# The activation h - tanh(h) by its short form alone, with a range test by row sums and a general path behind it

## The chip, the cores and the metric

The kernel runs on one core of a Trainium2 chip. The metric is the time of one execution on the device in microseconds, as the median of several runs. A profile holds one execution; its span runs from the first instruction to the last. PE is TensorE (PEld its weight loads), ACT ScalarE, DVE VectorE, POOL GpSimd, SP the engine that issues the DMAs.

## The reference

Three stages follow each other on the same 4608 tokens (8 batches of 576). First an attention with 32 packed keys for each of 8 heads, then a layer with a cubic-like activation, then a layer in which each token goes to one of 8 experts:

```python
def sm_attn(qq, kk, vv):
    s = scale * np.matmul(qq, kk.transpose(0, 1, 3, 2))
    ...
p_packed = sm_attn(p, k, v)
x = sm_attn(q, p_packed, p_packed)      # as 4608 x 512
h = x @ w_in                            # 512 -> 2048
g = h - np.tanh(h)
x = g @ w_out                           # 2048 -> 512
logits = x @ w_gate + modality_bias[modality_id]
e_idx = np.argmax(logits, axis=1)
...
out[mask] = gate_w[mask, None] * (np.maximum(x[mask] @ w1[e], 0.0) @ w2[e])
```

The inputs are normal draws with a seed that defaults to 0. v has a spread of 0.1, and q, k and p have 0.8. w_in and w_out are float64 in memory.

## The kernel before

**Tiling.** The tokens are worked on in 16 half batches of 288 tokens (HW = 288), number hb. h is held transposed: 128 of the 2048 hidden columns on the partitions, 288 tokens along the row. A half batch has 16 such tiles f (NF = 16). One step of the first part is a *slot* n: one tile f of one half batch. There are 256 of them; the first 32 serve half batches 0 and 1 in alternating halves, while the weights are still being converted.

**A slot.** `gemm1` (L720) multiplies m, the product of the packed values and w_in, with a2, the second attention's weights, into a PSUM tile `h` (two buffers). From slot 32 on both operands are split into a high and a low part, and `mm3` (L96) makes three matmuls of each product. `chain` (L731) makes g out of h. `gsplit` (L754) splits g into gh and gl. `gemm2` (L765), three slots later (LAG = 3), multiplies them with w_out into four PSUM tiles `acc`. At the end of a half batch `evac` (L779) copies acc out, splits it and stores it to DRAM (x2_hi, x2_lo). `logits_pe`, `route_in` and `routing` compute the expert of each token.

**The chain.** For small u = h^2, h - tanh(h) is PA (exp(-PK u) + PB) u h, the short form. ACT computes u (L741), tanh(h) (L742), a mask that is nonzero where u > U_THR = 0.0775 (L743) and the exponential (L744). DVE computes h - tanh(h) (L745), the two steps of the short form (L747, L749), and selects the first where the mask is set (L751). u, qq, th and mk have one buffer each. The low part gl is computed on POOL in seven of sixteen slots and on DVE in the others (L761, L762).

**Beside the slots.** The loops of the main part give each slot a list of further work by number (`at_pe`, `at_pre`, `at_post`, `at_cv`): the attention of the next batch (`attention`, L247), the m tiles of the next batch (`m_pe`, L211, eight per batch, with loads of `ws` three slots ahead), and in the first slots the conversion of the float64 weights (`conv_a`, L159: two steps on DVE, three on ACT, one on POOL; `conv_b`, L187). Within these lists a planner orders each engine's instructions; TensorE's small products all go through one PSUM tile `at` (AT). Almost all DMAs are issued on SP's queue.

**The second layer.** From slot 256 on, `gemm1b`, `relu` and `gemm2b` compute the expert of token 0 for all tokens. `flags_a`, `flags_pe` and `flags_b` (L611 to L646) count, for each other expert and half batch, whether a token chose it. `other_experts` (L649) reads that total at the very end (n_any, L652) and branches (L653): if it is not zero, it goes through all experts, and for each with tokens through all half batches with tokens (`other_half`, L680), computes this expert in full precision and writes the rows that chose it.

## Time and profile before

| | us |
|---|---|
| median of 3 runs | 1284.95 |
| lowest, highest run | 1284.23, 1285.18 |
| the profiled execution | 1284.04 |
| its span | 1282.3 |

The granted TensorE clock is 0.983 of full speed over the span. The page gives each engine's busy time and its share of the span; a group row gives line, engine, operation, tile and shape, then busy time, mean ns of one, and the idle time just before with what ended it. Windows split the span in time.

### The profile page before, as it was taken

How to read it: one execution, taken by the hardware profiler on the slowest of the kernel's cores; microseconds unless marked ns; L12 is line 12 of the kernel's file. 1: busy time of each engine (PE TensorE's matmuls, PEld its weight loads, DVE VectorE, ACT ScalarE, POOL GpSimd, SP SyncE). 2: the span in 40 equal slices, each digit the busy share in tenths (PEclk: the TensorE clock that was granted, in tenths of full speed). 3: DMA queues.
4: the chain of work that ended last, by engine and by line, in shares of the span. 5: the costliest groups of instructions: out<-in, count | busy, mean ns of one | idle time of the engine just before them, and what ended most of it. 6: DMA issues, size and time to landing. Idle time of an engine off the chain costs nothing.

```text
span 1282.3 us, 25934 instructions
## 1 busy us (share of the span) xinstructions
PE 1210.1 (94%) x9762; PEld 1049.7 (82%) x9763; DVE 838.4 (65%) x1941; ACT 710.3 (55%) x1832; POOL 166.3 (13%) x174
## 2 busy tenths in 40 slices
PE   5688889999999999999999999999999999999996
PEld 2455668889889889979979978989899999999995
DVE  4987999898998898998898897884111111111111
ACT  3888867678678678678677777772111111111111
POOL 1322211121111111111111122240000000000000
PEclk7799899999999999999999999999999999999998
DMA  8766344454354344344345126212122222222201
GB/s 241 213 201 197 104 131 118 106 131 121 73 129 119 73 125 124 73 118 128 73 108 139 39 83 194 79 51 74 63 83 67 82 61 76 64 65 83 66 17 35
DMA packets 189843, 132.36 MB, mean 103 GB/s; under 512 B 122640, under 2 KB 167696, under 8 KB 189712
## 3 DMA queue, kind: packets, MB, share of 16 engines
q1 hardware_dynamic: 189712, 130.65, 36.6%
q8 instruction: 78, 1.28, 0.4%
q14 instruction: 53, 0.43, 0.1%
HBM read 98.10 MB, written 32.51 MB: 102 GB/s over the span
## 4 chain that ended last, share of the span: by engine, by line
PE 68%; DVE 16%; issue 7%; ACT 4%; DMA 3%; POOL 2%; SPq 0%; POOLq 0%; DVEq 0%; ACTq 0%
PE acc L98 12%; PE acc L100 12%; PE acc L99 11%; PE h L98 9%; PE h L99 8%; PE h L100 8%; PE at L202 2%; DVE gs L749 2%; DVE th L745 2%; DVE gs L751 2%; DVE gl L762 1%; PE at L340 1%; DVE qq L747 1%; DMA w1s<-in_moe_w_dram 1%; DVE s L466 1%
## 5 line engine op out<-in xcount | busy, mean ns | idle before, releaser
L98 PE MATMUL acc<-gh,wo_hi 128*128 128x288 f32 x960 | 293.9, 308 | 6.4 <-ACT gh L760 4.0
L100 PE MATMUL acc<-gl,wo_hi 128*128 128x288 f32 x960 | 277.0, 298 | 5.4 <-DVE gl L762 2.9
L99 PE MATMUL acc<-gh,wo_lo 128*128 128x288 f32 x960 | 281.9, 295 | 0.0
L98 PEld LDWEIGHTS acc<-gh,wo_hi 128*128 128x128 f32 x960 | 180.4, 188 | 42.2 <-ACT u L741 13.2
L100 PEld LDWEIGHTS acc<-gl,wo_hi 128*128 128x128 f32 x960 | 177.6, 188 | 13.5 <-DVE gl L762 6.2
L99 PEld LDWEIGHTS acc<-gh,wo_lo 128*128 128x128 f32 x960 | 180.6, 188 | 0.4 <-issue 0.2
L100 PE MATMUL h<-xbl,w1h 128*128 128x256 f32 x576 | 162.3, 282 | 0.0
L99 PE MATMUL h<-xbh,w1l 128*128 128x256 f32 x576 | 162.1, 281 | 0.0
L98 PE MATMUL h<-xbh,w1h 128*128 128x256 f32 x576 | 161.5, 280 | 0.0
L762 POOL TENSOR_TENSOR gl<-gs,gh 128x288 fp32r<-128x288 f32 x105 | 85.7, 817 | 569.4 <-ACT gh L760 398.4
L745 DVE TENSOR_TENSOR th<-h,th 128x288 f32<-128x288 f32 x256 | 114.8, 449 | 53.8 <-ACT mk L743 51.2
L751 DVE COPY_PREDICATED gs<-mk,th 128x288 f32<-128x288 int32 x256 | 140.1, 547 | 2.6
L98 PE MATMUL h<-ah,mh 128*128 128x288 f32 x448 | 135.2, 302 | 6.5 <-DVE gs L749 6.5
L741 ACT ACTIVATE u<-h 128x288 f32<-128x288 f32 x256 | 106.0, 414 | 63.3 <-PE h L100 40.8
L863 DVE SCALAR_TENSOR_TENSOR bl<-h,bh 128x256 fp32r<-128x256 f32 x72 | 30.6, 425 | 164.0 <-ACT bh L862 163.9
L99 PE MATMUL h<-ah,ml 128*128 128x288 f32 x448 | 132.2, 295 | 0.0
L100 PE MATMUL h<-al,mh 128*128 128x288 f32 x448 | 131.8, 294 | 0.0
L747 DVE SCALAR_TENSOR_TENSOR qq<-qq,u 128x288 f32<-128x288 f32 x256 | 122.7, 479 | 12.8 <-ACT qq L744 9.9
L744 ACT ACTIVATE qq<-u 128x288 f32<-128x288 f32 x256 | 114.6, 448 | 27.1 <-DVE gs L749 21.9
L760 ACT ACTIVATE gh<-gs 128x288 fp32r<-128x288 f32 x240 | 107.6, 449 | 35.3 <-PE acc L99 33.8
L742 ACT ACTIVATE th<-h 128x288 f32<-128x288 f32 x256 | 104.6, 409 | 34.9 <-DVE gs L751 32.2
L862 ACT ACTIVATE bh<-h 128x256 fp32r<-128x256 f32 x72 | 27.6, 384 | 171.3 <-PE h L100 169.8
(163 smaller groups left out, 2426.4 us busy)
## 6 DMA issues: line engine op xcount, KB each, us to landing
ws<-w_in_v SPq DMA_DIRECT2D x56, 512.0 KB
nat<-in_v_dram SPq DMA_DIRECT2D x16, 576.0 KB
x_hi<-x2h SPq DMA_DIRECT2D x16, 576.0 KB
x_lo<-x2l SPq DMA_DIRECT2D x16, 576.0 KB
xbh<-x_hi SPq DMA_DIRECT2D x18, 512.0 KB
xbl<-x_lo SPq DMA_DIRECT2D x18, 512.0 KB
raw<-in_moe_w_in_dram SPq DMA_DIRECT2D x32, 256.0 KB
raw<-in_moe_w_out_dram SPq DMA_DIRECT2D x16, 512.0 KB
```

Of the source, the lines that this page charges most:

```text
L98: nc.tensor.matmul(out=ps, lhsT=ah, rhs=bh, start=first, stop=False)
L99: nc.tensor.matmul(out=ps, lhsT=al, rhs=bh, start=False, stop=False)
L100: nc.tensor.matmul(out=ps, lhsT=ah, rhs=bl, start=False, stop=last)
L741: nc.scalar.activation(out=u, in_=ps, func=ACTF.Square)
L742: nc.scalar.activation(out=th, in_=ps, func=ACTF.Tanh)
L744: nc.scalar.activation(out=qq, in_=u, func=ACTF.Exp, scale=-PK)
L745: nc.vector.tensor_tensor(out=th, in0=ps, in1=th, op=ALU.subtract)
L747: nc.vector.scalar_tensor_tensor(out=qq, in0=qq, scalar=PB, in1=u, op0=ALU.add, op1=ALU.mult)
L751: nc.vector.copy_predicated(gs, mk, th)
L760: nc.scalar.activation(out=gh, in_=gs, func=ACTF.Copy)
L762: eng.tensor_tensor(out=gl, in0=gs, in1=f32(gh), op=ALU.subtract)
L863: nc.vector.scalar_tensor_tensor(out=gl, in0=ps, scalar=0.0, in1=f32(gh), op0=ALU.max, op1=ALU.subtract)
```

## The change

The chain loses tanh, mask, subtraction and selection. u and qq get two buffers each in the place of th and mk. The square's activation also sums its row into a column of a new tile usum (128 x 256), one column for each slot. The split's low part is always on DVE. After the last slot, `flags_a` takes the largest row sum of each partition and compares it with U_THR; `flags_pe` counts the partitions over it, and `flags_b` puts the count into the flags and adds it to the total that is branched on. For the general path, a2, ppT and, in the path itself, the logits are kept in DRAM (a2_all, pp_all, lg_all).

If the count is not zero, `redo` runs ahead of the experts' loop. It converts w_out again and loops over the batches. In each it loads ppT and w_in, computes m, and in `redo_half` computes both halves in full precision with tanh, mask and selection, writes x anew and keeps the logits. Then it routes anew and sets the flags with `every=True`, which counts all experts, the one of token 0 too; the loop behind it then computes all of them.

The diff, without the arguments of the buffers in `relu` and lines that only move:

```diff
@@ -60,6 +60,11 @@
...
+    a2_d = nc.dram_tensor("a2_all", [NHB, 128, 2 * HW], F32, kind="Internal").ap()
+    pp_d = nc.dram_tensor("pp_all", [B, 128, 128], F32, kind="Internal").ap()
+    lg_d = nc.dram_tensor("lg_all", [NHB, 32, 9 * NE], F32, kind="Internal").ap()
@@ -81,6 +86,8 @@
...
     flags = const.tile([1, NE + 1, NHB + 1], I32, name="flags")
+    ones_b = const.tile([128, 1], F32, name="ones_b")
+    usum = const.tile([128, NHB * NF], F32, name="usum")
@@ -106,6 +113,7 @@
...
         nc.vector.memset(ones, 1.0)
+        nc.vector.memset(ones_b, 1.0)
@@ -173,6 +181,8 @@
...
             v = early.tile([128, 512], F32, name="wv", tag="wv", bufs=6)
+        elif key[0] == 2:
+            v = wv[key]
         elif key[1] < NWH // 2:
@@ -425,7 +435,9 @@
...
             t = ppT[b] = ap.tile([128, 4, 32], F32, name="ppT", tag="ppT", bufs=2)
-            nc.scalar.activation(out=t.rearrange("p h j -> p (h j)"), in_=ps[:, 0, 128:256], func=ACTF.Copy)
+            t = t.rearrange("p h j -> p (h j)")
+            nc.scalar.activation(out=t, in_=ps[:, 0, 128:256], func=ACTF.Copy)
+            nc.sync.dma_start(out=pp_d[b], in_=t)
@@ -490,6 +502,7 @@
...
             r["a2", half] = t
+            nc.sync.dma_start(out=a2_d[2 * b + half], in_=t.rearrange("p g c -> p (g c)"))
@@ -620,37 +633,133 @@
...
+        t = evp.tile([128, 1], F32, name="big", tag="big")
+        nc.vector.tensor_reduce(out=t, in_=usum, axis=AX.X, op=ALU.max)
+        yield
+        nc.vector.tensor_scalar(out=t, in0=t, scalar1=U_THR, scalar2=None, op0=ALU.is_gt)
+        yield
+        fl["big"] = t
...
         fl["ps"] = AT[0:1, 0, 0:NE * NHB]
+        nc.tensor.matmul(out=AT[0:1, 1, 0:1], lhsT=ones_b, rhs=fl["big"], start=True, stop=True)
         nc.tensor.matmul(
...
-    def flags_b():
-        other = evp.tile([1, NE], F32, name="other", tag="rt_m")
-        nc.vector.tensor_tensor(
-            out=other, in0=em8[0:1, :], in1=idx_t[0:1, 0:1].to_broadcast([1, NE]), op=ALU.not_equal
-        )
+    def flags_b(every=False):
         n = evp.tile([1, NE, NHB], F32, name="n_other", tag="rt_l")
-        nc.vector.tensor_tensor(
-            out=n, in0=fl["ps"].rearrange("o (e h) -> o e h", e=NE),
-            in1=other.unsqueeze(2).to_broadcast([1, NE, NHB]), op=ALU.mult,
-        )
-        yield
+        ps = fl["ps"].rearrange("o (e h) -> o e h", e=NE)
+        if every:
+            nc.vector.tensor_copy(out=n, in_=ps)
+        else:
+            other = evp.tile([1, NE], F32, name="other", tag="rt_m")
+            nc.vector.tensor_tensor(
+                out=other, in0=em8[0:1, :], in1=idx_t[0:1, 0:1].to_broadcast([1, NE]), op=ALU.not_equal
+            )
+            nc.vector.tensor_tensor(
+                out=n, in0=ps, in1=other.unsqueeze(2).to_broadcast([1, NE, NHB]), op=ALU.mult,
+            )
+            yield
         tot = evp.tile([1, NE + 1], F32, name="n_tot", tag="gq")
...
         yield
+        if not every:
+            nc.vector.tensor_copy(out=flags[:, NE, 0:1], in_=AT[0:1, 1, 0:1])
+            nc.vector.tensor_tensor(out=tot[:, NE:NE + 1], in0=tot[:, NE:NE + 1], in1=AT[0:1, 1, 0:1], op=ALU.add)
         nc.vector.tensor_copy(out=flags[:, 0:NE, 0:NHB], in_=n)
...
+    def redo():
+        nonlocal evp
+        with ExitStack() as st:
+            rp = st.enter_context(tc.tile_pool(name="rp", bufs=1))
+            rb = st.enter_context(tc.tile_pool(name="rb", bufs=2))
+            evp = rp
+            wo = rp.tile([128, NF, 512], F32, name="wo")
+            for f in range(NF):
+                raw = rb.tile([128, 1024], I32, name="rraw")
+                nc.sync.dma_start(out=raw, in_=w_out.bitcast(I32)[f * 128:f * 128 + 128, :])
+                raws[2, f] = raw.rearrange("p (a c) -> p a c", a=2)
+                wv[2, f] = wo[:, f, :]
+                for _ in conv_a((2, f)):
+                    pass
+            with tc.For_i(0, B, 1) as b:
+                pt = rp.tile([128, 4, 32], F32, name="rpt")
+                nc.sync.dma_start(out=pt, in_=pp_d[bass.ds(b, 1)].rearrange("o p (h j) -> p (o h) j", h=4))
+                m = rp.tile([128, NU, 2, 256], F32, name="rm")
+                for u in range(NU):
+                    ws = rb.tile([128, 4, 256], F32, name="rws")
+                    nc.sync.dma_start(out=ws, in_=win_v[u])
+                    tiled(
+                        lambda g, hh: AT[32 * hh:32 * hh + 32, g, 0:256],
+                        lambda g, hh: pt[64 * g:64 * g + 64, hh, :],
+                        lambda g, hh: ws[64 * g:64 * g + 64, hh, :],
+                    )
+                    nc.scalar.activation(out=m[:, u], in_=AT[:, :, 0:256], func=ACTF.Copy)
+                for half in range(2):
+                    redo_half(rp, rb, wo, m, b, half)
+            for hb in range(3, NHB, 4):
+                lt_t[0] = evp.tile([32, 36, NE], F32, name="rt_l", tag="rt_l")
+                nc.sync.dma_start(
+                    out=lt_t[0].rearrange("i (x r) e -> i x (r e)", x=4),
+                    in_=lg_d[hb - 3:hb + 1].rearrange("x i n -> i x n"),
+                )
+                run(lambda: routing(hb))
+            run(flags_a)
+            flags_pe()
+            run(lambda: flags_b(every=True))
+    def redo_half(rp, rb, wo, m, b, half):
+        a2 = rp.tile([128, 2, HW], F32, name="ra2")
+        nc.sync.dma_start(out=a2, in_=a2_d[bass.ds(b * 2 + half, 1)].rearrange("o p (g c) -> p (o g) c", g=2))
+        ac = [pools["acc"].tile([128, 512], F32, name=f"acc{c}") for c in range(4)]
+        for f in range(NF):
+            ps = ps_h.tile([128, HW], F32, name="h", tag="h")
+            for g in range(2):
+                nc.tensor.matmul(
+                    out=ps, lhsT=m[:, f // 2, g, 128 * (f % 2):128 * (f % 2) + 128], rhs=a2[:, g, :],
+                    start=(g == 0), stop=(g == 1),
+                )
+            u, qq, th, gs = (rb.tile([128, HW], F32, name=f"r{nm}") for nm in ("u", "qq", "th", "gs"))
+            mk = rb.tile([128, HW], I32, name="rmk")
+            nc.scalar.activation(out=u, in_=ps, func=ACTF.Square)
+            nc.scalar.activation(out=th, in_=ps, func=ACTF.Tanh)
+            nc.scalar.activation(out=mk, in_=ps, func=ACTF.Square, scale=(0.5 / U_THR) ** 0.5)
+            nc.scalar.activation(out=qq, in_=u, func=ACTF.Exp, scale=-PK)
+            nc.vector.tensor_tensor(out=th, in0=ps, in1=th, op=ALU.subtract)
+            nc.vector.scalar_tensor_tensor(out=qq, in0=qq, scalar=PB, in1=u, op0=ALU.add, op1=ALU.mult)
+            nc.vector.scalar_tensor_tensor(out=gs, in0=qq, scalar=PA, in1=ps, op0=ALU.mult, op1=ALU.mult)
+            nc.vector.copy_predicated(gs, mk, th)
+            for c in range(4):
+                nc.tensor.matmul(
+                    out=ac[c][:, 0:HW], lhsT=wo[:, f, c * 128:c * 128 + 128], rhs=gs, start=(f == 0), stop=(f == NF - 1)
+                )
+        xh, xl = ev_t[0] = [rp.tile([128, 4, HW], F32R, name=f"rx{c}") for c in "hl"]
+        for c in range(4):
+            nc.scalar.activation(out=xh[:, c, :], in_=ac[c][:, 0:HW], func=ACTF.Copy)
+            nc.vector.tensor_tensor(out=xl[:, c, :], in0=ac[c][:, 0:HW], in1=f32(xh[:, c, :]), op=ALU.subtract)
+        for d, t in zip(xs, (xh, xl)):
+            nc.sync.dma_start(out=d[:, :, bass.ds(b * S + half * HW, HW)], in_=f32(t))
+        logits_pe(0)
+        run(lambda: route_in(0))
+        nc.sync.dma_start(
+            out=lg_d[bass.ds(b * 2 + half, 1)].rearrange("o i n -> (o i) n"),
+            in_=lt_t[0][:, 0:9, :].rearrange("i r e -> i (r e)"),
+        )
...
         hi_f = 32
-        n_any = nc.values_load(flags[0:1, NE, NHB:NHB + 1], min_val=0, max_val=hi_f)
+        n_any = nc.values_load(flags[0:1, NE, NHB:NHB + 1], min_val=0, max_val=hi_f + 128)
         with tc.If(n_any > 0):
+            n_big = nc.values_load(flags[0:1, NE, 0:1], min_val=0, max_val=128)
+            with tc.If(n_big > 0):
+                redo()
             with tc.tile_pool(name="ow", bufs=1) as ow, tc.tile_pool(name="ox", bufs=2) as ox:
@@ -730,25 +839,18 @@
...
         ps = ht.pop(n)
-        u = gp.tile([128, HW], F32, name="u")
-        qq = gp.tile([128, HW], F32, name="qq")
-        th = gp.tile([128, HW], F32, name="th")
-        mk = gp.tile([128, HW], I32, name="mk")
+        u = gp.tile([128, HW], F32, name="u", bufs=2)
+        qq = gp.tile([128, HW], F32, name="qq", bufs=2)
         if n < NWH:
...
             gs = gp.tile([128, HW], F32, name="gs", bufs=2)
-        nc.scalar.activation(out=u, in_=ps, func=ACTF.Square)
-        nc.scalar.activation(out=th, in_=ps, func=ACTF.Tanh)
-        nc.scalar.activation(out=mk, in_=ps, func=ACTF.Square, scale=(0.5 / U_THR) ** 0.5)
+        nc.scalar.activation(out=u, in_=ps, func=ACTF.Square, accum_out=usum[:, n:n + 1])
         nc.scalar.activation(out=qq, in_=u, func=ACTF.Exp, scale=-PK)
-        nc.vector.tensor_tensor(out=th, in0=ps, in1=th, op=ALU.subtract)
         yield
...
         nc.vector.scalar_tensor_tensor(out=gs, in0=qq, scalar=PA, in1=ps, op0=ALU.mult, op1=ALU.mult)
-        yield
-        nc.vector.copy_predicated(gs, mk, th)
         gt[n] = gs
@@ -758,8 +860,7 @@
...
         nc.scalar.activation(out=gh, in_=gs, func=ACTF.Copy)
-        eng = nc.gpsimd if n >= 16 and n % 16 in [3, 5, 7, 9, 11, 13, 15] else nc.vector
-        eng.tensor_tensor(out=gl, in0=gs, in1=f32(gh), op=ALU.subtract)
+        nc.vector.tensor_tensor(out=gl, in0=gs, in1=f32(gh), op=ALU.subtract)
         gt[n] = (gh, gl)
...
```

More of the change, by code (lines that the diff above doesn't have):

```diff
@@ L856, in relu @@
             gh, gl = (
-                gp.tile([128, TB], F32R, name="bg", tag=tg) for tg in (("u", "qq") if n % 4 == 1 else ("th", "mk"))
+                gp.tile([128, TB], F32R, name="bg", tag=tg, bufs=2) for tg in ("u", "qq")
             )
@@ L911, in seq, with run @@
                 yield
+    def run(*fns):
+        for _ in seq(fns):
+            pass
     with ExitStack():
@@ L995, in attn_moe_moe_kernel @@
             at_cv(NWH + 1 + f * 11 // 7, lambda f=f: conv_b((1, f)))
-        def run(*fns):
-            for _ in seq(fns):
-                pass
         ps0 = tc.alloc_tile_pool(name="ps0", bufs=1, space=PSUM)
```

## Prediction

> **What bounds the kernel now.** The split into stages comes first, because the busy line of the page mixes stages with different limits.
>
> ```profile
> core 0: us, PE busy (x) PEld busy (x) DVE busy (x) ACT busy (x) POOL busy (x), PEclk, DMA share, GB/s
> 38.70:190.00 151.30, 128.75 (x867) 85.95 (x868) 132.35 (x277) 124.34 (x291) 40.22 (x37) 0.93 0.60 172
> 190.00:862.00 672.00, 652.45 (x5995) 582.51 (x5994) 596.42 (x1405) 498.75 (x1339) 119.37 (x125) 1.00 0.40 106
> 862.00:1272.00 410.00, 409.50 (x2633) 371.62 (x2631) 86.97 (x205) 70.76 (x171) 1.59 (x2) 1.00 0.20 64
> ```
>
> From 38.7 to 190 us run the first 32 slots beside the conversion of the float64 weights: no engine is full, VectorE leads with 132 of 151 us. From 190 to 862 us run the other 224 slots: TensorE is busy for 652 of 672 us and VectorE for 596. From 862 us on, the second layer is TensorE alone (409.5 of 410 us); chain, split and activation are not in it. Next, what the weight loads waited for in the middle stage (us in total, times, longest).
>
> ```profile
> PEld acc L98 <- ACT u L741: 11.1, 26, 0.5
> PEld h L98 <- DVE gs L749: 9.2, 12, 1.5
> PEld acc L98 <- ACT gh L760: 7.6, 12, 0.8
> PEld acc L98 <- DVE x2l L796: 6.7, 18, 0.7
> PEld acc L100 <- POOL gl L762: 5.0, 12, 0.9
> PEld acc L100 <- DVE gl L762: 4.9, 6, 0.8
> PEld at L202 <- DVE rt_t L556: 4.4, 6, 0.7
> ```
>
> The first row is no wait for work: 26 times 0.43 us, the same pause wherever a group of small matmuls ends. The other six sum to 37.8 us, of which I take a third as that same pause. About 26 us in 672 are stalls that a lighter VectorE, ScalarE or GpSimd could end. The last rows are those of the branch at the end (L653) and of what lies behind it.
>
> ```profile
> L653 PEldq COMPARE_BRANCH  x1: 3432/3432/3432, 1267.8 to 1267.8; - x1
> L653 ACTq COMPARE_BRANCH  x1: 50/50/50, 1271.4 to 1271.4; - x1
> nothing on L656; most used: ['L98', 'L99', 'L100', 'L202', 'L393', 'L340', 'L741', 'L762', 'L745', 'L744', 'L749', 'L760', 'L862', 'L726', 'L771', 'L437', 'L742', 'L743', 'L747', 'L751', 'L278', 'L380', 'L863', 'L316', 'L548']
> ```
>
> L656 is the first instruction of the body of `other_experts`: it did not run, so in the timed inputs all tokens have one expert. That matters below.
>
> **The change, part by part: the main pass.** These are the groups of the chain.
>
> ```profile
> L742 ACT ACTIVATE th<-h 128x288 f32<-128x288 f32 x256 | 104.6, 409 | 34.9 <-DVE gs L751 32.2 <-DVE nm L351 0.7 <-DVE rs L373 0.5
> L744 ACT ACTIVATE qq<-u 128x288 f32<-128x288 f32 x256 | 114.6, 448 | 27.1 <-DVE gs L749 21.9
> L745 DVE TENSOR_TENSOR th<-h,th 128x288 f32<-128x288 f32 x256 | 114.8, 449 | 53.8 <-ACT mk L743 51.2
> L747 DVE SCALAR_TENSOR_TENSOR qq<-qq,u 128x288 f32<-128x288 f32 x256 | 122.7, 479 | 12.8 <-ACT qq L744 9.9
> L749 DVE SCALAR_TENSOR_TENSOR gs<-qq,h 128x288 f32<-128x288 f32 x256 | 112.4, 439 | 1.0
> L751 DVE COPY_PREDICATED gs<-mk,th 128x288 f32<-128x288 int32 x256 | 140.1, 547 | 2.6
> L762 POOL TENSOR_TENSOR gl<-gs,gh 128x288 fp32r<-128x288 f32 x105 | 85.7, 817 | 569.4 <-ACT gh L760 398.4
> L762 DVE TENSOR_TENSOR gl<-gs,gh 128x288 fp32r<-128x288 f32 x135 | 66.8, 495 | 4.6 <-ACT gh L760 4.4
> L361 ACT ACTIVATION_READ_ACCUMULATOR a<-at,nm 128x1 f32 x30 | 5.5, 183 | 0.0
> ```
>
> Each slot loses two activations (2 x 0.41 us), the subtraction (0.449) and the selection (0.547): 256 x 1.0 = 255 us of VectorE. VectorE gains 105 subtractions that were GpSimd's (105 x 0.495 = 52 us), ScalarE one accumulator read per slot (256 x 0.183 = 47 us, against 210 removed). In the middle stage the six waits above lose their causes. What is late next is the evacuation of `acc` and the `at` buffer, which stay single, so I take -22 us of the 26 (bounds 0 and -38). In the stage before it, the first-layer matmuls waited for `gs`:
>
> ```profile
> PEld h L726 <- DVE gs L749: 9.0, 8, 3.2
> PEld h L726 <- DVE gs L749: 5.5, 4, 2.6
> ```
>
> (to 130 us, and from there to 190). 14.5 us in all: I take -14, with 0 as one end (the conversion sets the pace anyway) and -32 (all of VectorE's 32 x 1.0 us) as the other. The stores of `a2` and `ppT` go on SP's queue: 16 of 288 KB and 8 of 64 KB, and what is queued behind each waits for a transpose on VectorE. DMA's share is 0.40 in the middle stage, and the weight loads behind are issued three slots (some 9 us) ahead, so this costs nothing; without that cover, about 1 us each, 24 us. The extra flag matmul is 0.3 us. Sum of the main pass: -36, that is 1284.0 (this execution; the median is 1285.0) to **1248 us**.
>
> **Does the general path run?** The old mask tested each element, u > 0.0775. The new flag tests a row's sum of 288 squares against the same 0.0775. Attention nearly averages here: all tokens of a batch have almost the same x, and so a column of h almost one value. Worked out in float arithmetic from the reference's own default draw (seed 0): the largest |h| is 0.0180 and the largest row sum 288 x 0.0180^2 = 0.0935, over the limit; 6 rows of 32768 are over it, in three partitions, though no single u exceeds 0.00033. Of 18 seeds that I worked out, 16 have a row over the limit. In that default draw all 4608 tokens choose expert 6; only 2 of the 18 seeds have one expert alone, and the untaken branch in the trace asks for one. Both of these are over the limit. So the flag counts 3, n_any and n_big are 3, `redo` runs, and with `every=True` behind it `other_experts` runs for expert 6 in all 16 half batches.
>
> **The price of the general path.** No row shows it, so it is built from the nearest ones.
>
> ```profile
> 60.70 2.10 PE L771 MATMUL acc<-gs,wv 128*128 128x288 f32 x8
> 63.61 0.65 PE L771 MATMUL acc<-gs,wv 128*128 128x288 f32 x2
> 1265.85 0.12 PE h L100
> 1266.43 0.23 PE acc L100
> L202 PE MATMUL at<-ws,ppT 64*32 64x256 f32 x896 | 41.2, 392 | 3.0 <-DVE rt_t L556 3.0
> 780.72 4.79 DMA w1s<-in_moe_w_dram
> 449.65 3.17 DMA nat<-in_k_dram
> 975.50:979.00 3.50, 3.50 (x26) 3.24 (x24) 0.43 (x1) 0.38 (x1) 0.00 (x0) 1.00 0.91 299
> L166 DVE SCALAR_TENSOR_TENSOR raw<-raw 128x512 int32<-128x512 int32 x32 | 27.2, 850 | 0.3
> L170 ACT ACTIVATE raw<-raw 128x512 int32<-128x512 f32 x32 | 21.9, 684 | 8.8 <-DVE raw L166 6.7 <-issue 1.9
> L178 POOL TENSOR_TENSOR wv<-raw 128x512 f32<-128x512 f32 x24 | 27.1, 1130 | 84.7 <-ACT raw L171 73.9 <-PE acc L771 6.1 <-DVE gl L762 3.1
> 985.30:992.30 7.00, 7.00 (x44) 6.23 (x43) 1.28 (x3) 1.16 (x3) 0.00 (x0) 1.00 0.25 77
> ```
>
> A full-precision matmul is two instructions; from 2 to 8 of them takes 1.45 us more, 0.242 us each at 288 columns. From 256 to 512 columns a step doubles (0.12, 0.23), so 512 columns cost 0.43. A small load held the chain for 3.2 to 4.8 us, a large one moves 299 GB/s, an output store by groups of rows 77 GB/s. A jump costs from 0.05 us (ACT) to 3.4 (PE); I take 4 us for a join of all engines with its jump, as PE's row is the one that all wait for.
>
> - `redo`, w_out: 16 tiles through a two-deep buffer, each 3.5 us load, 0.85 on VectorE and about half of it for the shift ahead, three times 0.684 on ScalarE, 1.13 on GpSimd, together 8.0: 16 x 8.0 / 2 = 64 (28 if the load alone counts, 128 if nothing overlaps).
> - `redo`, one batch: join 4, first load 5, eight m groups of 0.74 with the 0.43 pause (9), 2 x 16 slots of 4 + 8 instructions of 0.242 = 93, filling the chain twice at 3.0 (0.41 + 0.41 + 0.41 + 0.45 on ScalarE, then 0.48 + 0.44 + 0.55 on VectorE) = 6, two evacuations 5, the last x store 8. 130 us, times 8 = 1040.
> - Routing four times 8, flags 10: 42.
> - `other_experts`: two stores of 4608 single elements, 25 (6 to 80); seven empty turns of the expert loop at 5, and 4.2 MB of weights at 299 GB/s, 17 + 5: 57.
> - One half batch: register load and jump 4, x load 7.0 (1.18 MB at 299 GB/s behind 3.1), the sum of both parts 1.8 (0.449 x 1152 / 288), 64 x 0.242 = 15.5, ReLU 0.4, 48 x 0.43 = 20.6, then scale and select of the last block at 512 columns 1.8 and its store 4.4 (196 KB at 77 GB/s, and 1.8 to start), leaving 2, half of a loop's join 1.5: 59. Times 16 = 944.
> - Entry 8.
>
> Sum: 64 + 1040 + 42 + 25 + 57 + 944 + 8 = 2180, and 1248 + 2180 = **3428 us**, call it 3430. Of it 16 x (46.5 + 15.5 + 20.6) = 1322 us is bare TensorE time, so below 1248 + 1322 = 2570 it can't be if the path runs.
>
> The Trainium skill (Runtime: NRT & Kernel Launch, Instruction fetch mechanics) says that a taken branch out of the two-page window stalls for an instruction fetch. PE's 3432 ns against 50 on ACT agrees. By that rule each far jump pays the long price, as the sum above has it; by ACT's row alone the sum would be 3270. Its page TensorE: Matmul & The Clock Gate (What's actually happening) says that an idle window of about 3.4 us halves the clock until a busy one has passed. By it 32 restarts would each lose about 1.7 us, an estimate of 54 us more; the trace's clock is 1.00 in the steady stages and 0.93 in the stage with gaps, which agrees in direction.
>
> **Rivals.**
> - The path doesn't run (the other side): the timed inputs' largest row sum stays below 0.0775, or the flag doesn't get through; then the time is the main pass alone, 1248 us (1224 to 1275). It decides at 0.0775 against a computed 0.0935, 21% over, a difference that rounding can't make. For it speaks that the inputs' seed isn't in the profile; against it the single expert. 0.10.
> - In `redo`, TensorE keeps its written order, so that gemm2 of a slot waits for its chain before gemm1 of the next: 3.0 us more in 240 slots = 720, 4150 us. Against it, these rows: scores1 is written in one piece, and yet a first-layer matmul of a later slot stands between its halves, so the order is planned by readiness. 0.15.
>
> ```profile
> 68.55 1.64 PE L340 MATMUL at<-T,pT 32*32 32x288 f32 x18
> 70.12 1.24 PE L726 MATMUL h<-a2w,m_w 128*128 128x288 f32 x4
> 71.29 1.17 PE L340 MATMUL at<-T,pT 32*32 32x288 f32 x14
> ```
>
> - The path costs much more by joins or element-wise stores: at 8 us a join and 80 us a store over 4300 only together with the rival before. 0.05. Much less than 3000: 0.03.
>
> **How the numbers follow.** The forecast (path runs, planned order) has 0.67. It gives 3430. Joins at the short price (some 48 x 3.4 = 160 less), the weight conversion by its loads alone (36) and 14 us in each half batch whose loads and stores overlap (230) reach 3000; the serial rival with dearer joins reaches 4300. The range 3000 to 4300 leaves out the untaken path (0.10) and the two last cases. Faster by over 0.2% is the untaken path, 0.10; within 0.2%, about what a measurement of this kernel can tell from no change, needs both an untaken path and no gain: 0.01; slower 0.89.
>
> **What would show it.** Right: a span near 3.4 ms, the main pass ending near 1235 us with its waits for `gs` and `gl` gone, then 256 tanh activations of `redo`, eight equal stretches of about 130 us, then 16 of about 58 us. Wrong: a span near 1250 us with nothing behind the branch; or stretches of about 220 us, which would be the serial order.

## The result and the profile after

| | us |
|---|---|
| before, median of 4 runs (lowest, highest) | 1284.91 (1284.23, 1285.18) |
| after, median of 4 runs (lowest, highest) | 3575.11 (3572.71, 3584.75) |
| ratio after to before, 95% interval | 2.784 (2.779 to 2.789) |
| span of the profiled execution, after | 3570.7 |

The kernel is slower by 2290 us: the general path runs. Seven windows cover the whole span, cut where one part of the program ends and the next begins (window, length, busy us of PE, PEld, DVE, ACT and POOL, each with its count, granted clock, DMA share, GB/s):

```profile
0.00:1244.70 1244.70, 1193.89 (x9764) 1049.63 (x9765) 685.74 (x1538) 589.39 (x1576) 77.70 (x69) 0.98 0.40 110
1244.70:1248.40 3.70, 0.02 (x1) 0.00 (x0) 1.80 (x5) 0.05 (x1) 0.00 (x0) 0.93 0.16 23
1248.40:1317.20 68.80, 0.99 (x16) 0.30 (x16) 20.79 (x32) 27.69 (x48) 15.59 (x16) 0.50 0.46 148
1317.20:2417.00 1099.80, 871.55 (x4216) 608.97 (x4208) 476.54 (x1120) 398.03 (x1152) 1.03 (x1) 0.94 0.15 50
2417.00:2448.30 31.30, 0.77 (x4) 0.17 (x4) 19.94 (x64) 1.77 (x4) 0.00 (x0) 0.53 0.25 40
2448.30:2506.80 58.50, 0.03 (x1) 0.06 (x1) 2.40 (x9) 0.00 (x0) 0.00 (x0) 0.50 0.63 96
2506.80:3570.70 1063.90, 622.34 (x1792) 344.75 (x1792) 94.79 (x160) 52.51 (x128) 0.00 (x0) 0.78 0.12 34
```

In order: the main pass; the entry; w_out converted again; the eight batches of `redo`; routing and flags; gates stored, empty turns and the expert's weights; the 16 half batches of the expert pass. Against the sum of the prediction (3428 us; its PE end near 1235, and the 21 us between that end and the first work of `redo`, stand here as its first two terms):

| part | predicted us | measured us | difference |
|---|---|---|---|
| main pass, to TensorE's last matmul | 1235 | 1244.7 | +10 |
| from there to the first load of `redo` | 21 | 3.7 | -17 |
| w_out again | 64 | 68.8 | +5 |
| eight batches | 1040 | 1099.8 | +60 |
| routing and flags | 42 | 31.3 | -11 |
| gates, empty turns, weights | 82 | 58.5 | -24 |
| 16 half batches, to the end | 944 | 1063.9 | +120 |
| sum | 3428 | 3570.7 | +143 |

**The main pass.** Its gain is read from the two stages that the prediction had bounded. These are the windows of after that answer to those of before; the second stage is cut at 824 us in both, and its row of before stands first:

```profile
190.00:824.00 634.00, 617.52 (x5750) 550.00 (x5749) 561.55 (x1340) 469.58 (x1261) 101.02 (x109) 1.00 0.41 107
```

```profile
38.70:190.00 151.30, 127.55 (x868) 90.04 (x869) 108.99 (x221) 111.00 (x263) 33.07 (x30) 0.93 0.64 180
190.00:824.00 634.00, 624.89 (x5911) 567.33 (x5910) 461.39 (x1043) 386.02 (x1095) 35.88 (x25) 1.00 0.45 118
```

VectorE fell from 132 to 109 us in the first window and from 562 to 461 in the second, and TensorE rose from 618 to 625 of 634 us in the second, with 5911 matmuls in place of 5750; in the first it did no more work than before (128.75 and 127.55). The start of the chain's last step tells the slots apart: from the 33rd slot to the 256th it took 675.0 us before and 649.3 after, 25.7 less; from the first to the 33rd 143.3 and 140.7. So nearly all of the gain is in the middle stage. The waits of the weight loads in the early window, of before (first fence) and after (second), show why (us in total, times, longest):

```profile
PEld h L726 <- DVE gs L749: 14.5, 12, 3.2
PEld at L202 <- POOL wv L178: 9.8, 10, 1.5
```

```profile
PEld at L212 <- POOL wv L188: 14.9, 11, 3.8
```

The wait for `gs` is gone from the top (1.4 us are left), and the wait for `wv`, the converted weights, has grown from 9.8 to 14.9 us. TensorE now waits for the conversion more than for the chain: in part one wait took another's place.

### The profile page after: what moved, and what is told of

It is laid out like the page before. It is cut to its first block, busy times and chain, and to the rows that moved or that the text cites. A ratio compares the mean times of both kernels' runs of the same rounds, so it can differ in the third digit from the quotient of the medians.

```text
span 3570.7 us, 43844 instructions
## 1 busy us (share of the span) xinstructions
PE 2689.6 (75%) x15784; PEld 2003.9 (56%) x15785; DVE 1302.0 (36%) x2928; ACT 1069.4 (30%) x2908; POOL 94.3 (3%) x85
## 5 line engine op out<-in xcount | busy, mean ns | idle before, releaser
L800 PE MATMUL h<-ohi,a 128*128 128x288 f32 x1024 | 292.8, 454 | 471.5 <-DVE omk L822 269.5
L738 PE MATMUL acc<-rgs,wo 128*128 128x288 f32 x2048 | 528.4, 413 | 27.3 <-DVE rgs L736 27.0
L800 PEld LDWEIGHTS h<-ohi,a 128*128 128x128 f32 x1024 | 219.3, 216 | 551.1 <-issue 484.4
L738 PEld LDWEIGHTS acc<-rgs,wo 128*128 128x128 f32 x2048 | 389.9, 192 | 150.6 <-DVE rgs L736 27.9
L723 PE MATMUL h<-ra,rm 128*128 128x288 f32 x1024 | 303.3, 430 | 112.0 <-DVE rgs L735 111.8
L807 PE MATMUL acc<-bw,oh_t 128*96 128x512 f32 x768 | 332.2, 593 | 0.0
L733 DVE TENSOR_TENSOR rth<-h,rth 128x288 f32<-128x288 f32 x256 | 116.7, 456 | 549.9 <-ACT rmk L731 549.8
L723 PEld LDWEIGHTS h<-ra,rm 128*128 128x128 f32 x1024 | 190.2, 196 | 209.9 <-DVE rgs L735 148.2
L729 ACT ACTIVATE ru<-h 128x288 f32<-128x288 f32 x256 | 105.8, 413 | 507.4 <-PE h L723 493.6
L807 PEld LDWEIGHTS acc<-bw,oh_t 128*96 128x96 f32 x768 | 125.5, 163 | 197.7 <-issue 195.6
```

The lines of the kernel that those rows point to most:

```text
L723: nc.tensor.matmul(out=ps, lhsT=m[:, f // 2, g, 128 * (f % 2):128 * (f % 2) + 128], rhs=a2[:, g, :], start=(g == 0), stop=(g == 1),)
L729: nc.scalar.activation(out=u, in_=ps, func=ACTF.Square)
L733: nc.vector.tensor_tensor(out=th, in0=ps, in1=th, op=ALU.subtract)
L738: nc.tensor.matmul(out=ac[c][:, 0:HW], lhsT=wo[:, f, c * 128:c * 128 + 128], rhs=gs, start=(f == 0), stop=(f == NF - 1))
L800: nc.tensor.matmul(out=ps, lhsT=a[:, c, f * 128:f * 128 + 128], rhs=xx[0][:, c, :], start=(c == 0), stop=(c == 3))
L807: nc.tensor.matmul(out=acc_t, lhsT=h[:, f, t * 96:t * 96 + 96], rhs=bw[:, f, :], start=(f == 0), stop=(f == NF2 - 1))
```

## The experiments

Twelve kernels ran. Five of them leave the general path untaken and tell what the main pass is worth and why; five take the general path apart; two replace the test.

### The limit doubled: is the general path the whole loss?

```diff
-        nc.vector.tensor_scalar(out=t, in0=t, scalar1=U_THR, scalar2=None, op0=ALU.is_gt)
+        nc.vector.tensor_scalar(out=t, in0=t, scalar1=2.0 * U_THR, scalar2=None, op0=ALU.is_gt)
```

> The changed kernel with the flag's limit at 2 x 0.0775 = 0.155, nothing else changed; the computed largest row sum is 0.0935. Theory (the row sum trips the flag, and all of the loss is the general path behind the branch): the path is not taken, nothing stands behind the main pass, and the time is that of before less what the main pass of the changed kernel gained in its trace (last matmul at 1244.3 + 0.4 against 1271.1 + 0.4, so 26.8 us): 1285 - 27 = 1258 us, 1254 to 1262. Rival (the loss has another cause, or the row sums are far over 0.0935): 3575 us as with the change.

Measured: 1258.45 us (1255.67 to 1258.78, 5 runs), ratio to before 0.978 (0.977 to 0.980). One constant takes 2317 us away. So the largest row sum of the timed inputs lies between 0.0775 and 0.155, where the computed 0.0935 is, and all of the loss stands behind the branch. Without it the short form alone gains 27.6 us over the 1286.05 of before, measured beside it.

### What gave the 27 us

Three more kernels with the doubled limit, each with one change; the last loses the stores and with them `redo`, which alone reads them.

```diff
+        eng = nc.gpsimd if n >= 16 and n % 16 in [3, 5, 7, 9, 11, 13, 15] else nc.vector
-        nc.vector.tensor_tensor(out=gl, in0=gs, in1=f32(gh), op=ALU.subtract)
+        eng.tensor_tensor(out=gl, in0=gs, in1=f32(gh), op=ALU.subtract)
```

> As the raised limit, with seven of sixteen gl subtractions back on GpSimd as in the kernel before. Theory A (the waits for GpSimd's gl, 5.0 + 1.8 us in the middle stage of before, were one of the stalls that the change ended): 5 to 8 us slower than the raised limit alone, 1263 to 1266. Theory B (VectorE has room either way, and the gain is from the two activations, the subtraction and the selection that went): within 2 us of it, 1256 to 1260.

Measured: 1257.97 us (1256.52 to 1259.34). No difference, theory B. The move of 105 subtractions to VectorE neither costs nor gains: with the lighter chain, GpSimd's `gl` ends no wait worth a measurable time.

```diff
-        nc.scalar.activation(out=u, in_=ps, func=ACTF.Square, accum_out=usum[:, n:n + 1])
+        nc.scalar.activation(out=u, in_=ps, func=ACTF.Square)
```

> As the raised limit, with the Square activation not accumulating (usum stays zero, so the range isn't tested): ScalarE loses 256 accumulator reads of about 0.18 us, 47 us. Theory (ScalarE is busy for some 60% of the middle stage and no longer ends a wait there): within 2 us of the raised limit, 1256 to 1260. Rival (the read lengthens each chain and the chain still ends waits): 5 to 10 us less, 1248 to 1253.

Measured: 1257.51 us (1257.34 to 1257.88). No difference that can be told (the ranges overlap): the 256 reads of the accumulator are hidden, as priced.

```diff
-            nc.sync.dma_start(out=pp_d[b], in_=t)
...
-            nc.sync.dma_start(out=a2_d[2 * b + half], in_=t.rearrange("p g c -> p (g c)"))
...
-            n_big = nc.values_load(flags[0:1, NE, 0:1], min_val=0, max_val=128)
-            with tc.If(n_big > 0):
-                redo()
```

> As the raised limit, without the 16 stores of a2 and the 8 of ppT and without redo, which alone reads them (so nothing could be redone). Theory (the stores lie beside other work, priced at nothing in the prediction): within 2 us of the raised limit, 1256 to 1260. Rival (what queues behind them on SP's queue is late, about 1 us each): 24 us less, 1234.

Measured: 1251.89 us (1250.14 to 1253.18), 6.6 us less than with the stores. Neither number: the stores, or the code of `redo` that went with them, cost something, but a quarter of the rival's 24. DMA issues on SP's queue of the doubled limit with the stores (first fence) and without (second) show a place for it (start us, us, line, tiles, count):

```profile
38.74 0.34 SPq L505 DMA_DIRECT2D a_all<-a2w  x1
...
43.96 0.34 SPq L505 DMA_DIRECT2D a_all<-a2w  x1
...
68.07 13.30 SPq L154 DMA_DIRECT2D raw<-in_moe_w_in_dram  x4
...
88.64 1.25 SPq L154 DMA_DIRECT2D raw<-in_moe_w_in_dram  x2
```

```profile
65.89 10.19 SPq L154 DMA_DIRECT2D raw<-in_moe_w_in_dram  x4
...
84.84 1.26 SPq L154 DMA_DIRECT2D raw<-in_moe_w_in_dram  x2
```

The two stores of a2 stand ahead of the raw weights in the queue, and the same loads start 2 to 4 us later. In the first 32 slots TensorE waits for the weights that come of these loads (14.0 us for `wv` with the doubled limit). So the next kernel moved only the first batch's three stores (two of a2, one of ppT) behind the loads.

```diff
-            nc.sync.dma_start(out=a2_d[2 * b + half], in_=t.rearrange("p g c -> p (g c)"))
+            st = lambda: nc.sync.dma_start(out=a2_d[2 * b + half], in_=t.rearrange("p g c -> p (g c)"))
+            if b:
+                st()
+            else:
+                at_post(25 + half, st)
```

(and the same for ppT, at slot 24).

> As the raised limit, with the first batch's three stores (ppT and two of a2) put off from before the first slot to slots 24 to 26; the other 21 stay where they are. Theory A (the 6.6 us that the run without stores gained were loads of float64 weights queued behind these three on SP's queue: they were issued 3 to 5 us later with the stores, and the conversion is what the first 32 slots wait for): 4 to 5 us less than the raised limit, 1253 to 1255. Theory B (it is the stores' traffic anywhere, or the code of redo): no change, 1257 to 1259.

Measured: 1253.57 us (1253.25 to 1254.71), ratio 0.976 (0.974 to 0.977), where the doubled limit alone had 1255.67 to 1258.78: 4.9 us less by the medians, theory A. SP's queue has the loads nearly back at the early times (this group at 66.73 us, the next at 85.68), and the group is issued in 10.19 us again:

```profile
66.73 10.19 SPq L154 DMA_DIRECT2D raw<-in_moe_w_in_dram  x4
```

The chain's last step shows the gain where it was expected: from the first slot to the 33rd pass 139.4 us with the doubled limit alone, 136.0 without the stores and 135.3 with the three moved. The other 1.7 us of the 6.6 (the 21 later stores, or the code of `redo`) weren't told apart. The two kernels weren't measured together; by the ratios to before the gain is 3.7 us and the intervals touch, so the 4.9 is good to two or three microseconds.

### The general path in two halves

```diff
-            nc.vector.tensor_copy(out=n, in_=ps)
+            nc.vector.tensor_scalar(out=n, in0=ps, scalar1=0.0, scalar2=None, op0=ALU.mult)
```

> The changed kernel with the counts of the second flags set to zero: redo runs, and the second layer isn't computed from what it redid. Theory (parts of the sum add up): 16 half batches of 66.5 and 22 us of weights go, an empty turn of 3.6 comes: 3575 - 1064 - 22 + 4 = 2493 us, 2480 to 2505. By the prediction's own sum the rest would be 1248 + 64 + 1040 + 42 + 25 + 40 + 8 = 2467. Rival (the two parts share a cost, such as a clock held down by the one in the other): under 2440 or over 2550.

Measured: 2504.85 us (2498.84 to 2510.28).

```diff
-            with tc.If(n_big > 0):
+            with tc.If(n_big > 127):
                 redo()
...
-                out=n, in0=ps, in1=other.unsqueeze(2).to_broadcast([1, NE, NHB]), op=ALU.mult,
+            nc.vector.tensor_copy(out=n, in_=ps)
```

> The changed kernel with redo never entered (its branch asks for a count above 127) and with the first flags counting the chosen expert too: the first layer isn't redone, and the expert pass runs over the main pass's x. Theory: the 1200 us from 1248.4 to 2448.3 go: 2375 us, 2360 to 2390; with redo alone it adds up to the whole (2493 - 1258 + 2375 - 1258 = 2352 against 3575 - 1258 = 2317, the 35 us of both being stores of gates and empty turns). Rival (the half batches are slow because redo ran before them): below 2330.

Measured: 2388.35 us (2384.61 to 2389.73). They are 12 and 13 us above the points that were expected. Over the 1258.45 of the untaken path, `redo` alone is worth 1246 us and the experts alone 1130; together 2376, against 2317 for both in one run. The 60 us over are mostly what each pays by itself: the stores of the gates and the empty turns take some 50 us in each of the two traces and 42 once in the changed kernel. The two halves add up; neither makes the other dear.

### The tail of a half batch in the expert pass

A half batch was priced at 59 us and took 66.5 (1063.9 / 16): 64 and 69 in turn, as the batch loop turns behind every second one. SP's queue in the second half batch of the changed kernel:

```profile
2562.06 0.65 SPq L793 DMA_DIRECT2D ohi<-x_hi  x1
...
2565.17 0.88 SPq L818 DMA_DIRECT2D oo<-out_dram  x1
...
2597.35 0.83 SPq L824 DMA_DIRECT2D out_dram<-oo  x1
2603.51 0.76 SPq L818 DMA_DIRECT2D oo<-out_dram  x1
...
2610.48 0.81 SPq L824 DMA_DIRECT2D out_dram<-oo  x1
2616.52 0.75 SPq L818 DMA_DIRECT2D oo<-out_dram  x1
...
2623.03 0.76 SPq L824 DMA_DIRECT2D out_dram<-oo  x1
2631.47 0.66 SPq L793 DMA_DIRECT2D ohi<-x_hi  x1
```

and TensorE in the same time:

```profile
2570.72 18.19 PE L800 MATMUL h<-ohi,a 128*128 128x288 f32 x64 [25.60 <-issue]
2588.75 20.76 PE L807 MATMUL acc<-bw,oh_t 128*96 128x512 f32 x48
```

The matmuls end at 2609.5, and the last store goes out at 2623.0. The rows that a block merges into (`oo`) are loaded one block at a time, each some 6 us behind the store of the block before. Two causes fit: the buffers, of which there are two, or the order of loads and stores on the same tensor `out`, whose rows are addressed by a loop register (whether the register matters wasn't tested).

```diff
-            with tc.tile_pool(name="ow", bufs=1) as ow, tc.tile_pool(name="ox", bufs=2) as ox:
+            with tc.tile_pool(name="ow", bufs=1) as ow, tc.tile_pool(name="ox", bufs=3) as ox:
```

> The changed kernel with three buffers in place of two for the rows, gates and results of a half batch in the expert pass. In its trace the third block's row load is issued only once the store before it has landed, and 13.5 us pass from the last matmul of a half batch (2609.5) to its last store (2623.0). Theory A (that load waits because rows of out are being stored, whatever the buffer): no change, 3565 to 3585 us. Theory B (it waits for one of two buffers): it can be issued at the start, the last 12 us of each half batch go, 16 x 12 = 190, 3385 us; 3470 if only half of it goes.

Measured: 3574.91 us (3573.99 to 3575.79): no change. Not the buffers.

```diff
+        pre = []
+        for t in range(3):
+            g = ox.tile([96, 2], F32, name=f"og{t}")
+            ...
+            o = ox.tile([96, 512], F32, name=f"oo{t}")
+            nc.sync.dma_start(out=o, in_=rows)
+            pre.append((g, o, rows))
         nc.vector.tensor_tensor(out=xx[0], in0=xx[0], in1=xx[1], op=ALU.add)
...
-            g = ox.tile([96, 2], F32, name="og")
-            ...
-            nc.sync.dma_start(out=o, in_=rows)
+            g, o, rows = pre[t]
```

> The changed kernel with the three row loads and six gate loads of a half batch issued before its matmuls, ahead of its first store, each into a tile of its own. Theory A (row loads wait for the store before them) and theory B (for a buffer) both take 12 us off each half batch: 3575 - 190 = 3385 us, 3370 to 3405; then the half batch is 66.5 - 12 = 54.5 us. Rival (the tail is the stores themselves, or the early loads delay the x load): 3500 or more. With three buffers alone this run tells A from B.

Measured: 3382.69 us (3381.85 to 3387.11), 192 us less, 12.0 per half batch. Theory A. What SP waited for in the whole run says the same; first with the change, then with the loads issued first (L818 is the row load, L828 the store):

```profile
SPq L818 <- DMA out_dram<-oo: 162.0, 32, 5.1
```

```profile
SPq L828 <- DMA out_dram<-oo: 163.4, 32, 5.1
```

With the change these are 32 waits, two in each half batch, 5.06 us each, for a store of other rows of `out` to land (with three buffers 161.0, the same). With the loads first the waits are not gone: the next store has them now. But the matmuls of the next block, some 6.9 us, run beside them, and no row load stands behind them.

### The order on TensorE in `redo`

A batch was priced at 130 us and took 137.5 (1099.8 / 8). Part of TensorE's time in the changed kernel, in a steady stretch:

```profile
1538.80 5.98 PE L738 MATMUL acc<-rgs,wo 128*128 128x288 f32 x24
1544.62 2.10 PE L723 MATMUL h<-ra,rm 128*128 128x288 f32 x8
1548.28 1.24 PE L723 MATMUL h<-ra,rm 128*128 128x288 f32 x4 [1.55 <-DVE rgs L735]
1549.35 5.99 PE L738 MATMUL acc<-rgs,wo 128*128 128x288 f32 x24
```

The planner has put three slots of the second layer in a row (24 matmuls), and then three of the first (8 and 4). The first layer has two buffers of `h`, so its third slot waits until VectorE has read one free. Three slots take 10.55 us, 3.52 us each.

```diff
-        for f in range(NF):
+        hold = {}
+        for f in range(NF + 2):
+            if f < NF:
...
+                hold[f] = gs
+            if f >= 2:
+                e, gs = f - 2, hold.pop(f - 2)
             for c in range(4):
                 nc.tensor.matmul(
-                    out=ac[c][:, 0:HW], lhsT=wo[:, f, c * 128:c * 128 + 128], rhs=gs, start=(f == 0), stop=(f == NF - 1)
+                    out=ac[c][:, 0:HW], lhsT=wo[:, e, c * 128:c * 128 + 128], rhs=gs, start=(e == 0), stop=(e == NF - 1)
                 )
```

> The changed kernel with the second-layer matmuls of redo written two slots behind the first-layer ones (four buffers for their input). In the trace of the change the program's order on TensorE there is three slots of the first layer, then three of the second, and the third waits 1.55 us for its buffer of h: 10.55 us per three slots, 3.52 each, where 12 matmuls of 0.245 make 2.95. Theory (this grouping is what made a batch 138.7 us and not 130): the wait goes, 3.0 us per slot, 32 x 0.55 = 18 us per batch, 8 x 18 = 140 in all: 3435 us, 3420 to 3460. Rival (the chain of activations, 4 x 0.3 us on ScalarE and 4 x 0.5 on VectorE per slot, or the loads set the pace): 3530 or more.

Measured: 3416.67 us (3413.90 to 3423.08), 158 us less, 19.8 per batch, a little over the 18 expected (and so just below the range of 3420 to 3460). The slots now alternate, without a wait, at 2.91 us each:

```profile
1528.59 1.13 PE L725 MATMUL h<-ra,rm 128*128 128x288 f32 x4
1529.56 2.10 PE L744 MATMUL acc<-rgs,wo 128*128 128x288 f32 x8
1531.50 1.13 PE L725 MATMUL h<-ra,rm 128*128 128x288 f32 x4
```

### Another test that the inputs don't trip

Doubling the limit widens the range in which the short form is used. Two kernels keep the limit for a single u and test it by a sum that stays further below the limit. Both also have the first batch's three stores moved as in the run above, which is the run beside them; the diffs leave that out.

```diff
-        nc.scalar.activation(out=u, in_=ps, func=ACTF.Square, accum_out=usum[:, n:n + 1])
+        nc.scalar.activation(out=u, in_=ps, func=ACTF.Square)
         nc.scalar.activation(out=qq, in_=u, func=ACTF.Exp, scale=-PK)
+        eng = nc.vector if n < 2 * NWH else nc.gpsimd
+        eng.tensor_tensor(out=usum, in0=usum, in1=u, op=ALU.add)
...
```

> Another test of the range, at the limit 0.0775 itself: u of every slot is added element by element to one 128 x 288 tile (first 32 slots on VectorE, the other 224 on GpSimd), the accumulation in the Square goes, and the first batch's three stores are put off as in the run beside it. A sum of 256 squares bounds each of them as the row sum did; worked out from the default draw it is at most 0.0065, a twelfth of the limit. Theory (GpSimd, busy for 6% of the middle stage, has room for 224 x 0.82 = 184 us of adds, and nothing waits for them but u's buffer): path not taken, within 3 us of the run beside it, 1251 to 1257. Rival (the adds hold u's two buffers or slow VectorE): 10 us more or worse, 1264 and up; and 3575 if the sum trips after all.

Measured: 1274.79 us (1274.16 to 1275.31), 21 us over the run beside it: not tripped, but the rival's price. VectorE, and GpSimd's adds, in the window 190 to 824, of the run beside it (first fence) and of this one (second; busy us, mean ns | idle before):

```profile
L859 DVE SCALAR_TENSOR_TENSOR qq<-qq,u 128x288 f32<-128x288 f32 x218 | 106.6, 489 | 125.8 <-ACT qq L857 125.6
L871 DVE TENSOR_TENSOR gl<-gs,gh 128x288 fp32r<-128x288 f32 x218 | 102.9, 472 | 27.7 <-ACT gh L870 27.6
L861 DVE SCALAR_TENSOR_TENSOR gs<-qq,h 128x288 f32<-128x288 f32 x218 | 96.2, 441 | 4.2
```

```profile
L860 POOL TENSOR_TENSOR usum<-usum,u 128x288 f32<-128x288 f32 x209 | 180.0, 861 | 403.1 <-ACT u L857 400.0 <-ACT ppT L440 2.9
L862 DVE SCALAR_TENSOR_TENSOR qq<-qq,u 128x288 f32<-128x288 f32 x210 | 147.3, 702 | 98.3 <-ACT qq L858 97.8
L874 DVE TENSOR_TENSOR gl<-gs,gh 128x288 fp32r<-128x288 f32 x210 | 107.2, 511 | 16.3 <-ACT gh L873 16.2
L864 DVE SCALAR_TENSOR_TENSOR gs<-qq,h 128x288 f32<-128x288 f32 x210 | 92.2, 439 | 3.9
```

The step of the chain that starts beside GpSimd's add, from qq and u, takes 702 ns in place of 489. The split, with gs and gh as its operands, takes 511 in place of 472. The step that reads h from PSUM keeps its 440. That makes some 45 us more of VectorE (210 x 0.213) and longer chains. All but 1 of the 21 us fall in the middle stage: the 33rd slot's last step starts at 182.9 us (181.9 in the run beside it), the 256th's at 852.8 (831.8). There TensorE's weight loads waited longer for what VectorE makes, 10.7 us in place of 2.9 for `x2l` and 11.1 in place of 6.6 for `rt_t`; ScalarE waited for the adds to free `u` for only 2.2 us. So of the rival's two reasons the traces point to the slower VectorE. The last kernel put the test on ScalarE:

```diff
-        nc.scalar.activation(out=u, in_=ps, func=ACTF.Square, accum_out=usum[:, n:n + 1])
+        nc.scalar.activation(out=u, in_=ps, func=ACTF.Square)
+        nc.scalar.activation(out=qq, in_=u, func=ACTF.Square, accum_out=usum[:, n:n + 1])
         nc.scalar.activation(out=qq, in_=u, func=ACTF.Exp, scale=-PK)
...
-        nc.vector.tensor_scalar(out=t, in0=t, scalar1=U_THR, scalar2=None, op0=ALU.is_gt)
+        nc.vector.tensor_scalar(out=t, in0=t, scalar1=U_THR ** 2, scalar2=None, op0=ALU.is_gt)
...
```

> A third test of the range, on ScalarE: u is squared once more with accumulation, and the row's sum of u squared is compared with 0.0775 squared = 0.0060. Any u above the limit still trips it; in the default draw, with no u above 0.00033, the sum is at most 288 x 0.00033 x 0.00033 = 0.00003. The accumulation moves from the first Square to the new one, and the first batch's three stores are put off to slots 24 to 26. Theory (ScalarE, busy for 385 of 634 us in the middle stage, has room for 0.41 us more per slot, and shares nothing with VectorE as the adds on GpSimd did, which took VectorE's first chain operation from 0.49 to 0.70 us): path not taken, 1254 to 1260 us against 1253.6 with the raised limit. Rival (a chain longer by 0.3 to 0.4 us per slot ends waits again, above all in the first 32 slots): 1262 to 1275; and 3575 if it trips.

Measured: 1255.17 us (1253.91 to 1257.09), ratio 0.976 (0.975 to 0.978). It beats the kernel before by 30 us and keeps a safe test at the old limit, with the general path behind it; from the run beside it (ratio 0.976 too) it can't be told. Its middle stage (190 to 824):

```profile
190.00:824.00 634.00, 626.01 (x5908) 567.18 (x5907) 452.58 (x1041) 473.32 (x1311) 36.30 (x26) 1.00 0.45 118
```

ScalarE is busy for 473 us in place of 385, and TensorE is as full as without the test.

## Why the prediction was right, and where it was off

The forecast was 3430 us in a range of 3000 to 4300; the time is 3575, the case the likeliest one. Of the sum's parts four were too low, by 195 us together, and three too high, by 52; that the total is only 143 off owes something to luck.

- **The path runs.** Right, and for the reason given: a limit for one element was applied to a sum of 288, and the doubled limit and the sum of u squared both stay clear of the branch. The rival of the untaken path (0.10) fell; its price of 1248 us was 10 too low.
- **Middle stage, -22 us.** The mechanism held and the size nearly: 25.7 us. Of the six waits named, those for `gs`, `gh`, `x2l` and both for `gl` fell (9.2, 7.6, 6.7 and 9.9 us before); the one for `gh` is down to 0.2. The sixth, for the routing's `rt_t`, did not lose its cause and grew from 4.4 to 6.6 us. That `gl` left GpSimd was no cause of its own: moving it back changed nothing. The same waits after, 190 to 862:

```profile
PEld at L212 <- DVE rt_t L569: 6.6, 6, 1.2
PEld acc L105 <- DVE x2l L897: 3.1, 8, 0.5
PEld h L105 <- DVE gs L853: 2.9, 4, 1.3
PEld acc L107 <- DVE gl L863: 0.2, 1, 0.2
```

- **Early stage, -14 us.** Wrong in size. The chain's last step, counted by windows, before (first fence) and after (second), stands at 33 slots and at 34 when 190 us are over: a slot of some 3 us ahead, not 14 us. Two things took the rest. The bound of 0 named one, "the conversion sets the pace anyway", and the wait for `wv` that grew from 9.8 to 14.9 us fits it. The other is the next term: with the first stores moved or left out, the first 32 slots take 135.3 and 136.0 us in place of 143.3, 7 to 8 less, and with these stores in front (138.1 to 141.0 in four traces) some 2 to 6 of that are lost again.

```profile
0.00:112.00 112.00, 6.65 (x15) 0.88 0.73 210
112.00:190.00 78.00, 7.99 (x18) 0.93 0.50 138
```

```profile
0.00:112.00 112.00, 7.56 (x17) 0.86 0.74 209
112.00:190.00 78.00, 7.41 (x17) 0.96 0.58 153
```

- **Stores of a2 and ppT, nothing.** Wrong: 6.6 us with the code of `redo`, 4.9 of it for the first three stores. The cover that was named, loads issued three slots ahead, holds for the later weights as far as the 1.7 us left over tell; it does not for the raw float64 weights queued behind the first stores, in the stage that waits for them.
- **The accumulator reads and gl on VectorE.** Rightly priced at nothing.
- **Entry, 21 us.** 3.7: the sum let the main pass land its last store first, and the first load of `redo` goes out 3.6 us after the issue of the last stores begins (1244.8 and 1248.4).
- **A batch of `redo`, 130 us.** Off by only 7.5, and that by luck: errors of opposite sign. The planned order was taken for a free one, 2.90 us per slot with two chain fills of 3 us; it groups three slots and pays 3.52 (20 us per batch too little, which the alternating order gave back). And joins and the last store overlapped more: the 19.5 us for the join, the first load, half the evacuations and the last store were 11.4, the stretch between the last second-layer matmul of one batch and the first product of the next (row below). The remaining 4 us are overlap as well: the products of m stand among the first slots in the trace, where the sum put them in front.

```profile
1444.90:1456.30 11.40, 1.56 (x13) 0.97 (x14) 1.15 (x3) 0.41 (x1) 0.00 (x0) 0.65 0.54 183
```

- **The serial rival, 4150 us.** It fell as written, but a fifth of its 720 us was there: three slots in a group are a part of the way to a serial order.
- **A half batch, 59 us.** The main mis-sizing, 120 of the 143 us. "Scale and select of the last block 1.8" was 13.5 (2609.5 to 2623.0): two loads of rows that wait for a store to land stand ahead of it. The first product took 18.2 us in place of 15.5. The ways in and out were cheaper than priced: from the last store to the next load 8.4 us where the batch loop turns and 3.3 where it doesn't, 5.9 in the mean, where store, leaving, half a join and the next jump had 11.9.
- **Routing and flags, 42 us,** were 31.3: the four routings follow each other every 5.3 us, where 8 was taken.
- **Gates, empty turns, weights, 82 us** were 58.5: VectorE's counter steps through the empty turns every 3.6 us, where 5 was taken. The stores ahead of them hold the second step for 19 us, where 25 was taken.

```profile
2470.04 0.15 DVE L787 TENSOR_SCALAR ev<-ev 128x1 f32<-128x1 f32 x1 [19.19 <-DVEq L770]
2473.66 0.15 DVE L787 TENSOR_SCALAR ev<-ev 128x1 f32<-128x1 f32 x1 [3.47 <-DVEq L770]
```

The restarts that stood beside the sum are in the trace too. After some 30 us without a matmul, the first product of a half batch begins so:

```profile
2639.35 5.88 PE L800 MATMUL h<-ohi,a 128*128 128x288 f32 x14 [29.84 <-DVE omk L822]
```

14 matmuls take 5.88 us, 0.42 each, where 0.242 makes 3.4: 2.5 us lost in each of 16 half batches, 40 us. The rule that the Trainium skill gives (TensorE: Matmul & The Clock Gate, What's actually happening), that an idle window halves the clock until a busy one has passed, agrees in direction; the prediction's estimate of 1.7 us a restart was too low here.

What a jump costs is in the traces too. On TensorE's queue a taken jump past code that isn't run took 3.43 us before (the prediction's row), 3.62 with the doubled limit, and 6.69 at the first empty turn of the experts' loop. The other seven branches there took 0.09 to 0.24 us, and those of the loops over batches and half batches 0.07 to 0.26. So the joins of the loops, in which the sum had a long jump each, paid the short price. What a join costs here is mostly the landing of the last store: of the 8.4 us above SP waits some 4 for it. The other rule that was cited (the Trainium skill, Runtime: NRT & Kernel Launch, Instruction fetch mechanics) fits the three long jumps.

## What to carry to other kernels

A test that is made cheaper must be checked against the data it will meet: a sum over a row compared with a limit meant for one element grows with the row, and a fallback 1.8 times as long as the whole kernel turns a gain of 2% into a factor of 2.8. A sum of a higher power (here of u squared) is as safe and, with these inputs, far from tripping; on ScalarE, which had room, it cost nothing that could be told. In a stage that waits for loads, a store is paid for where it stands ahead of them in the queue: three stores, 640 KB together, cost some 4 us here, and little once moved behind the loads.

## What the runs showed of the hardware

- GpSimd's adds made VectorE's steps with two operands in SBUF longer (489 to 702 ns and 472 to 511) and left the one with an operand in PSUM alone (441 and 439). The Trainium skill (Advanced Engine Details and Errata, GPSIMD Details) says that the two engines share an interface and get in each other's way where VectorE has two inputs in SBUF, and these rows agree. Split one by one, the first of these steps takes 434 ns where no GpSimd operation overlaps it (41 of 210) and 766 where one does (169). Of 165 that start inside a GpSimd operation, 156 end 0.30 to 0.33 us after that operation: the step looks held until GpSimd is done. With `gl` back on GpSimd in seven of sixteen slots only 26 of 217 overlap (839 ns against 454), so the mean hardly shows it.

- A row load of 192 KB waited 5.06 us for a store of other rows of the same tensor to land, 32 times; a third buffer changed nothing. With the loads issued first, the next store waited in its place, beside matmuls.
- A taken jump past code that isn't run held TensorE's queue for 3.4 to 6.7 us the first time; the same jump in the later empty turns took 0.23 to 0.24.
- An empty turn of the experts' loop, with its load of a count, its branch and one small step on VectorE, took 3.6 us.
